# Phases and coarse decays of an S4D convolution kernel as one row-tiled product

## The chip, the cores and the metric

The kernel runs on one core of a Trainium2 chip. The metric is the device time of one execution in microseconds; before the change it was 622.47 us, the median of three runs (621.3 to 626.9). TensorE multiplies, VectorE (DVE), ScalarE (ACT) and GpSimd (POOL) do element-wise work, SyncE (SP) issues nearly all transfers.

## The reference

Two branches of the same width are computed in float32 and mixed by a gate; L = 2048 steps, D = 640 channels, N = 128 modes, Dff = 1728.

```
g = sigmoid((u * gate_w).sum(-1))
dt = exp(log_dt);  A = -exp(log_A_real) + 1j*A_imag;  C = (C_real + 1j*C_imag) * dt
K[d, l] = 2 * Re( sum_n C[d, n] * exp(A[d, n] * dt[d] * l) )
a = causal convolution of u with K over l (by FFT) + u * D_skip
b = relu(x @ w1) @ w2
out = g * a + (1 - g) * b
```

## The kernel before

**Three kinds of work share TensorE.** The feed-forward branch (PSUM tile `pf`, called fill below) is computed in three parts of w1 and w2, each operand split into a high and a low half: products of 512 columns into the hidden layer, products of 320 columns out of it. Generation builds the filters K. The convolution (PSUM tile `pc`) transforms filters and input, multiplies and transforms back; it can only open when generation is over and its memory is free.

**Generation** goes through the 640 channels in 40 groups of 16. For each channel, step l is split as a coarse step of 32 and a fine rest, so that the exponential is a product of few values. Each channel has eight rows of parameters in tile `PS` (high and low halves of the phase per step, its offset, the decay, the size), 16 channels by 8 rows filling its 128 partitions; the modes are its columns. A visit of group c multiplies `PS` (stationary) by a table `tg` that holds the step numbers, spread so that each row only meets the columns of its own channel (`spread`, line 952). Before the change a visit is five products of 512 columns: two for the phases (`phases`, line 1018, tile `pg`: 16 channels of 64 values, two PSUM banks), two for the coarse decays (`exponents`, line 1041, tile `px`, the same size, two banks) and one for the fine decays (tile `pe`, 16 by 32, one bank).

Then ACT rounds the phases to an integer (`cs<-pg`), DVE subtracts it (`sn<-pg,cs`, line 1035) and takes the magnitude, ACT takes the exponential of the fine decays (`me<-pe`) and the coarse ones (`mg<-px`, line 1059), loads its other table and takes sine and cosine; DVE multiplies these into factors (`factors`, line 1075). Two groups at a time are then multiplied with each other (`taps`, tile `pk`, 128 small products), turned by DVE into `kt` and stored. The program has one `pk` for each of 20 pairs of groups.

**The convolution** takes 128 channels at a time, i = 0 to 4: a transform of the filter and of the input (tables `tf`, 64x64 tiles of TensorE's array), a second one (`tm`, 64x32 tiles), products by ACT, DVE and POOL, the inverse (`inv2`, table `tn`, 32x64 tiles), two copies by ACT (`back`), eight transposes by DVE (`relay`, line 1331), the last transform (`inv1`, table `tw`) and multiplication by the gate (ACT, tile `yo`).

**Mixing.** `CG` (line 23) has one entry for each of eight row blocks g of 256 steps. For the first CG[g] of the five channel blocks, the branch b of row block g takes the finished a (`joined`, `with_last`); for the others, b is stored to `py`, and a takes it when it is ready (POOL adds `yj` or `xu` to `yo`).

**The order of the work** is made when the program is built: a planner (`Plan.run`, line 226) has for each task an engine, an estimated duration, its dependencies, tokens of the buffers that it takes (`tok`) and a rank, and writes each engine's instructions in the order that comes out. Each engine runs its own in that order; only waits on others move them in time. TensorE changes between modes ('f' for full products, 't' and 'c' for tiles), which the planner prices. The layer below adds the waits between engines from the tiles that instructions share.

Of the kernel before, what the change touches and what calls it, by code (L numbers as in the profile page):

```python
# [10 lines left out]
F32 = mybir.dt.float32  # L11
F32R = mybir.dt.float32r
I32 = mybir.dt.int32
AF = mybir.ActivationFunctionType
# [5 lines left out]
NT = D // 128  # L20
TWO_PI = 2 * math.pi
PARTS = (5, 5, 4)
CG = (0,0,0,0,1,2,5,5)
FIRST = 7
SPIN = 6
S4R = 3
# [22 lines left out]
TGA = 4  # L49
# [4 lines left out]
GPR = 1  # L54
# [16 lines left out]
def slots():  # L71
    return np.concatenate([np.arange(32, 64), np.arange(31, -1, -1)])
# [5 lines left out]
def tables():  # L78
    a = np.arange(64)
    k1 = 2 * np.arange(32)[None, :] + np.arange(2)[:, None]  # L80
    al = 2 * np.pi * (k1[..., None] + 0.25) * a / 64
    f1 = np.stack([np.cos(al), np.sin(al)]).transpose(3, 1, 0, 2).reshape(64, 128)
    w = np.stack([np.cos(al), np.sin(al)], axis=1) / 2048
    b = np.arange(32)
    om = 2 * np.pi * (k1[:, :, None, None] + 0.25 + 64 * b[None, None, :, None]) * b / 2048
    c, s = np.cos(om), np.sin(om)
    m = np.zeros((2, 2, 32, 32, 2, 32))
    n = np.zeros((4, 32, 8, 2, 2, 2, 32))
    for p in range(2):
        ct, st = c[p].transpose(2, 0, 1), s[p].transpose(2, 0, 1)  # L90
        m[p, 0, :, :, 0], m[p, 0, :, :, 1] = ct, st
        m[p, 1, :, :, 0], m[p, 1, :, :, 1] = -st, ct
        for g in range(32):
            ck, sk = c[p, g], s[p, g]
            n[g % 4, :, g // 4, p, 0] = np.stack([ck, -sk], axis=1)
            n[g % 4, :, g // 4, p, 1] = np.stack([sk, ck], axis=1)


    tg = np.zeros((16, 8, 176))
    tg[:, :2, :32], tg[:, :2, 32:64], tg[:, 2:4, :32] = b, 32 * b + 16, 1  # L100
    tg[:, 4:6, 64:128], tg[:, 4:6, 128:160], tg[:, 6:, 128:160] = 32 * slots(), b, 1
    tg[np.arange(16), :, 160 + np.arange(16)] = 1
    f = lambda x: np.ascontiguousarray(x.astype(np.float32))
    return dict(t_g=f(tg.reshape(128, 176)), t_f1=f(np.tile(np.stack([f1, f1[slots()]], axis=1), (2, 1, 1))), t_w=f(w.reshape(128, 64)),
                t_m=f(m.reshape(128, 32, 64)), t_n=f(n.reshape(128, 8, 2, 2, 64)))


# [245 lines left out]
class Kernel:  # L353
# [30 lines left out]
    def feed_forward(self):  # L384
# [276 lines left out]
        def with_y(g, q_, qld):  # L661
            n, ts = CG[g], []
            for t in range(2):
# [6 lines left out]
        def joined(g, t, q_, dep):  # L670
            b, m, ts = 2 * g + t, min(CG[g], 4), []
            if m:
# [64 lines left out]
        for p, n in enumerate(PARTS):  # L737
# [4 lines left out]
            for k, g in enumerate(order):  # L742
# [84 lines left out]
    def params(self):  # L827
        tc, nc, io, A = self.tc, self.nc, self.io, self.plan.add
        V, S, P, D_ = self.V, self.S, self.P, self.D
        tl, last = {}, {}  # L830
# [66 lines left out]
        R = lambda f: (lambda V: f(V, *T_()))  # L897
# [48 lines left out]


        def steps_in():
            tl['tgs'] = self.prm.tile([128, 176], F32, name="tgs")
            D_.dma_start(tl['tgs'], io['t_g'])  # L950

        def spread(ds):
            def go():
                a, b = self.tg[:, :2048].rearrange("p (x d j) -> p d x j", x=2, j=64), self.tg[:, 2048:].rearrange("p (d j) -> p d j", j=32)
                for d in ds:
                    m = tl['tgs'][:, 160 + d:161 + d]
                    S.mul(a[:, d], tl['tgs'][:, :128].rearrange("p (x j) -> p x j", x=2), m)
                    S.mul(b[:, d], tl['tgs'][:, 128:160], m)
            return go
        a = A('SP', 'tg', 0.62, steps_in, [self.prm0], kb=88, rank=TGR)  # L960
        if TGR > 5:
            self.late_loads.append(a)
        for d in range(0, 16, 2):
            self.tg_done.append(A('ACT', 'tg', 1.1, spread(range(d, d + 2)), [a], rank=TGA))
        return [*done, *self.tg_done]

    def ssm(self, C=16):
        tc, nc, io, A, tok, ring = self.tc, self.nc, self.io, self.plan.add, self.plan.token, self.plan.ring
        V, S, P, D_ = self.V, self.S, self.P, self.D
        Q, n = C // 4, D // C  # L970
# [7 lines left out]
        self.tg = gk.tile([128, 2560], F32R, name="tg")  # L978
# [13 lines left out]
        st = {}  # L992
# [4 lines left out]
        opened = self.prm_shut = A('PY', 'open', 0, go, self.params())  # L997
        self.prm_open = opened
        R, rows = {}, {}
# [12 lines left out]
                rows[c + k] = a, r_  # L1012

        tasks, f = {}, {}
        I = lambda x: x.bitcast(I32)


        def phases(c):
            p_, s_ = tok('pg'), tok('sc')
            rd, r_ = rows[c]  # L1020

            def pe():
                p = self.psg.tile([128, 4, 256], F32, name="pg")
                pf = p.rearrange("p d j -> p (d j)")
                st['pg'] = pf.rearrange("p (d j) -> p d j", j=64)
                for h in range(2):
                    x = slice(h * 512, h * 512 + 512)
                    self.E.matmul(pf[:, x], R[c], self.tg[:, x], start=True, stop=True)

            def whole():  # L1030
                st['sc', c] = [st['gp'].tile([128, C, 64], F32, name=k, bufs=5) for k in ("sn", "cs")]
                S.copy(I(st['sc', c][1]), st['pg'])
            a = visit[c, 1] = A('PE', None, 0.46, pe, [rd, opened, *self.tg_done], take=[p_], use=[r_], rank=GPR, mode='f')
            b = acts[c, 0] = A('ACT', None, 0.97, whole, [a], take=[s_], use=[p_], rank=2)
            d = A('DVE', 'g1', 1.14, lambda: V.tensor_sub(st['sc', c][0], st['pg'], I(st['sc', c][1])), [b],
                  use=[p_, s_], rank=G1R)
            e = A('DVE', 'g1', 0.62, lambda: V.tensor_scalar(I(st['sc', c][1]), I(st['sc', c][0]), 0x7fffffff, None,
                                                             op0=ALU.bitwise_and), [d], use=[s_], rank=G1R, port=True)
            tasks[c] = dict(s=s_, abs=e)

        def exponents(c):
            p_, m_ = tok('px'), tok('mg')
            rd, r_ = rows[c]

            def pe():
                p = self.psg.tile([128, 4, 256], F32, name="px")
                pf = p.rearrange("p d j -> p (d j)")
                st['px', c] = pf.rearrange("p (d j) -> p d j", j=64)
                for h in range(2):
                    x = slice(h * 512, h * 512 + 512)  # L1050
                    self.E.matmul(pf[:, x], R[c], self.tg[:, 1024 + h * 512:1536 + h * 512], start=True, stop=True)
                q = st['pe', c] = self.psg.tile([128, C, 32], F32, name="pe")
                self.E.matmul(q.rearrange("p d j -> p (d j)"), R[c], self.tg[:, 2048:], start=True, stop=True)

            def exps(k):
                def go():
                    if k:
                        st['mg', c] = st['gp'].tile([128, C, 64], F32, name="mg", bufs=4)
                        S.activation(st['mg', c], st.pop(('px', c)), AF.Exp)
# [13 lines left out]
            tasks[c].update(m=m_, exps=[d, b], trig=[x, y])  # L1073
# [65 lines left out]
        visit, acts = {}, {}  # L1139
# [16 lines left out]
        for p in range(n // 2 + 1):  # L1156
            c = 2 * p
# [349 lines left out]
```

## Time and profile before

| | before |
|---|---|
| median of 3 runs | 622.47 us |
| the profiled execution | 632.85 us, span 631.1 us |
| TensorE busy | 609.0 us (97%), 7864 matmuls |
| VectorE busy | 507.9 us (80%) |
| ScalarE busy | 399.0 us (63%) |
| GpSimd busy | 92.4 us (15%) |
| granted TensorE clock, mean | 0.992 |
| first product of generation, last `pk` product begins | 82.7 us, 402.4 us |
| last product with `tw` begins | 608.3 us |

A TensorE row's duration runs from its start to a modelled end, and neighbours overlap; what a product costs is read from the distance of starts. The span is from the first to the last instruction; the profiled execution's own time has 1.8 us around it. Names such as `pf<-xx,w1h` are out<-in by the program's tile names.

### The profile page before, as it was taken

How to read it: one execution, taken by the hardware profiler on the slowest of the kernel's cores; microseconds unless marked ns; L12 is line 12 of the kernel's file. 1: busy time of each engine (PE TensorE's matmuls, PEld its weight loads, DVE VectorE, ACT ScalarE, POOL GpSimd, SP SyncE). 2: the span in 40 equal slices, each digit the busy share in tenths (PEclk: the TensorE clock that was granted, in tenths of full speed). 3: DMA queues.
4: the chain of work that ended last, by engine and by line, in shares of the span. 5: the costliest groups of instructions: out<-in, count | busy, mean ns of one | idle time of the engine just before them, and what ended most of it. 6: DMA issues, size and time to landing. Idle time of an engine off the chain costs nothing.

```text
span 631.1 us, 18316 instructions
## 1 busy us (share of the span) xinstructions
PE 609.0 (97%) x7864; PEld 481.6 (76%) x7864; DVE 507.9 (80%) x794; ACT 399.0 (63%) x579; POOL 92.4 (15%) x133
## 2 busy tenths in 40 slices
PE   7999989999999999999999999999979999989997
PEld 5998969888988988988988988755656465656656
DVE  5998559898999889999999998568676757746842
ACT  6578369997999888788789796023225342342470
POOL 0000000000000000000000000007060180361744
PEclk9999989998999999999999999999999999999999
DMA  9993933913656435535442243781543534563343
GB/s 292 386 371 116 406 102 115 301 58 109 195 184 242 153 108 205 153 112 177 133 144 81 64 162 116 234 339 30 194 127 126 183 103 136 185 221 102 115 149 119
DMA packets 54153, 108.05 MB, mean 171 GB/s; under 512 B 5432, under 2 KB 29880, under 8 KB 53176
## 3 DMA queue, kind: packets, MB, share of 16 engines
q1 hardware_dynamic: 53848, 106.63, 50.4%
q8 instruction: 62, 1.02, 0.7%
q10 hardware_dynamic: 224, 0.25, 0.1%
q14 instruction: 19, 0.16, 0.1%
HBM read 67.79 MB, written 39.06 MB: 169 GB/s over the span
## 4 chain that ended last, share of the span: by engine, by line
PE 78%; DVE 11%; DMA 5%; ACT 3%; issue 2%; POOL 0%; SPq 0%; DVEq 0%; ACTq 0%
PE pf L322 47%; PE pc L322 18%; PE pk L322 6%; PE pg L322 3%; PE px L322 2%; PE pe L322 1%; DMA ws<-in_B_w_dram 1%; DVE hwl L322 1%; DVE mg L322 1%; DVE sn L322 1%; DVE G L322 1%; DMA ps<-hl 1%; DMA xu<-in_x_dram 1%; DMA ws<-in_w_dram 1%; DMA PS<-ps 1%
## 5 line engine op out<-in xcount | busy, mean ns | idle before, releaser
L322 PE MATMUL pf<-xx,w1h 128*128 128x512 f32 x560 | 175.5, 399 | 1.7 <-DVE w1h L322 1.0
L322 PEld LDWEIGHTS pf<-xx,w1h 128*128 128x128 f32 x560 | 102.6, 189 | 37.2 <-issue 12.6
L322 PE MATMUL pf<-xx,w1l 128*128 128x512 f32 x260 | 102.1, 393 | 0.0
L322 ACT COPY ku<-pc 128x512 f32<-128x512 f32 (+1 forms) x60 | 43.8, 758 | 74.0 <-PE pc L322 63.4
L322 POOL TENSOR_TENSOR ku<-ku 128x256 f32<-128x256 f32 x80 | 56.2, 744 | 86.2 <-DVE ku L322 56.8
L322 POOL TENSOR_TENSOR kt<-kt,dsk 128x8 f32<-128x8 f32 x20 | 9.3, 466 | 393.0 <-DVE kt L322 211.6
L322 DVE STREAM_TRANSPOSE ku<-pc 128x512 f32<-128x512 f32 x80 | 50.8, 687 | 15.4 <-PE pc L322 15.2
L322 DVE TENSOR_TENSOR ku<-pc,ku 128x512 f32<-128x512 f32 x80 | 52.8, 686 | 11.0 <-ACT ku L322 9.6
L322 PE MATMUL pf<-w2l,hh 128*128 128x320 f32 x192 | 59.2, 312 | 1.9 <-issue 1.9
L322 PE MATMUL pf<-w2h,hh 128*128 128x320 f32 x192 | 59.7, 315 | 0.8 <-DVE q L322 0.8
L322 PE MATMUL pf<-w2h,hwh 128*128 128x320 f32 x192 | 59.7, 312 | 0.7 <-ACT hwh L322 0.7
L322 PE MATMUL pf<-w2l,hwh 128*128 128x320 f32 x192 | 59.9, 313 | 0.0
L322 PE MATMUL pf<-w2h,hwl 128*128 128x320 f32 x192 | 58.1, 316 | 1.9 <-DVE hwl L322 1.9
L322 ACT CAST cs<-pg 128x1024 int32<-128x1024 f32 x40 | 40.4, 1010 | 29.5 <-PE pg L322 29.4
L322 PEld LDWEIGHTS pf<-xx,w1l 128*128 128x128 f32 x260 | 49.0, 188 | 11.0 <-DVE w1l L322 0.3
L322 DVE TENSOR_TENSOR sn<-pg,cs 128x1024 f32<-128x1024 f32 x40 | 48.6, 1215 | 7.5 <-ACT cs L322 7.4
L322 ACT ACT_TABLE_LOAD x42 | 53.9, 1283 | 0.7
L322 DVE TENSOR_TENSOR mg<-mg,cs 128x1024 f32<-128x1024 f32 x40 | 49.0, 1224 | 2.9 <-ACT cs L322 1.0
L322 PE MATMUL pf<-w2h,hl 128*128 128x320 f32 x160 | 48.1, 317 | 0.0
L322 ACT ACTIVATE cs<-cs,half_pi 128x1024 f32<-128x1024 f32 x40 | 45.7, 1142 | 0.0
L322 PE MATMUL pc<-ku,tm 64*32 64x256 f32 x1280 | 42.9, 392 | 2.7 <-issue 2.4
L322 ACT ACTIVATE mg<-px 128x1024 f32<-128x1024 f32 x40 | 41.3, 1033 | 1.8 <-PE pk L322 1.8
(151 smaller groups left out, 1260.4 us busy)
## 6 DMA issues: line engine op xcount, KB each, us to landing
xx<-xt SPq DMA_DIRECT2D x24, 640.0 KB, 4.7
xt<-xx SPq DMA_DIRECT2D x16, 640.0 KB, 8.8
part<-q SPq DMA_DIRECT2D x16, 640.0 KB, 3.3
q<-part SPq DMA_DIRECT2D x16, 640.0 KB, 4.9
xl<-in_u_r_dram SPq DMA_DIRECT2D x16, 320.0 KB, 3.1
kd<-kt SPq DMA_DIRECT2D x80, 64.0 KB, 2.5
xu<-in_u_b_dram SPq DMA_DIRECT2D x5, 1024.0 KB, 4.9
xu<-in_x_t_dram SPq DMA_DIRECT2D x6, 640.0 KB, 6.8
```

What stands on the lines that cost most here:

```text
L322: self._last = self._tc.keep_in_program_order(f(*a, **k))
```

## The change

The sixteen channels of a group stand as four sets of four, each set on 32 partitions of `PS`. The table `tg` shrinks from 2560 to 1024 columns: columns 0 to 255 hold the phase steps of four channels, 256 to 511 the coarse decay steps, and every set of 32 rows finds its own four channels there; columns 512 to 1023 hold the fine decays as before. A visit is now four products of 32 rows, 128 columns of weights and 512 moving columns, each on its own quarter of the array's rows and into its own PSUM bank, then the one product for `pe`. Tile `pg` has four banks; in each, the first half is phases, the second coarse decays. Tile `px` is gone; `pg` alone takes the four banks that both had. The token of the old `px` is taken together with that of `pg`. The planner is told 0.26 us and mode 'g' for the four products and 0.24 us for the fifth. The table is written by 20 ACT instructions in place of 32. `CG[6]` goes from 5 to 3. The rest of the program's text is unchanged, but the planner lays it out anew.

```
-CG = (0,0,0,0,1,2,5,5)
+CG = (0, 0, 0, 0, 1, 2, 3, 5)
...
-    tg = np.zeros((16, 8, 176))
+    tg = np.zeros((16, 8, 180))
...
+    tg[np.arange(16), :, 176 + np.arange(16) % 4] = 1
...
-                    m = tl['tgs'][:, 160 + d:161 + d]
-                    S.mul(a[:, d], tl['tgs'][:, :128].rearrange("p (x j) -> p x j", x=2), m)
-                    S.mul(b[:, d], tl['tgs'][:, 128:160], m)
+                    if d < 4:
+                        S.mul(a[:, d], tl['tgs'][:, :128].rearrange("p (x j) -> p x j", x=2), tl['tgs'][:, 176 + d:177 + d])
+                    S.mul(b[:, d], tl['tgs'][:, 128:160], tl['tgs'][:, 160 + d:161 + d])
...
         def phases(c):
             p_, s_ = tok('pg'), tok('sc')
+            px_ = pxs[c] = tok('px')
...
-                p = self.psg.tile([128, 4, 256], F32, name="pg")
-                pf = p.rearrange("p d j -> p (d j)")
-                st['pg'] = pf.rearrange("p (d j) -> p d j", j=64)
-                for h in range(2):
-                    x = slice(h * 512, h * 512 + 512)
-                    self.E.matmul(pf[:, x], R[c], self.tg[:, x], start=True, stop=True)
+                p = self.psg.tile([128, 4, 512], F32, name="pg")
+                st['pg'], st['px', c] = p[:, :, :256], p[:, :, 256:]
+                for m in range(4):
+                    x = slice(32 * m, 32 * m + 32)
+                    self.E.matmul(p[:, m], R[c][x], self.tg[x, :512], start=True, stop=True)
...
-            a = visit[c, 1] = A('PE', None, 0.46, pe, [rd, opened, *self.tg_done], take=[p_], use=[r_], rank=GPR, mode='f')
+            a = visit[c, 1] = A('PE', None, 0.26, pe, [rd, opened, *self.tg_done], take=[p_, px_], use=[r_], rank=GPR, mode='g', n=4)
...
-                p = self.psg.tile([128, 4, 256], F32, name="px")
...
-                    self.E.matmul(pf[:, x], R[c], self.tg[:, 1024 + h * 512:1536 + h * 512], start=True, stop=True)
...
-            a = visit[c, 2] = A('PE', None, 0.69, pe, [rd, opened, *self.tg_done], take=[p_], use=[r_], rank=GPR, mode='f')
+            a = visit[c, 2] = A('PE', None, 0.24, pe, [rd, opened, *self.tg_done], use=[p_, r_], rank=GPR, mode='f', n=1)
```

In the order of the built programs, three places matter. First TensorE, a visit in the middle of generation; before:

```order
L322 MATMUL pf<-xx,w1h_1657 128x512 x2
L322 MATMUL pf<-xx,w1l_1658 128x512
L322 MATMUL pg<-tg,PS 128x512 x2
L322 MATMUL px<-tg,PS 128x512 x2
L322 MATMUL pe<-tg,PS 128x512
L322 MATMUL pf<-xx,w1h_1683 128x512 x2
```

A visit in the changed program, also between rows of fill:

```order
L323 MATMUL pf<-w2l_2148,hwh_2213 128x320
L323 MATMUL pf<-w2h_2147,hwl_2214 128x320
L323 MATMUL pg<-tg,PS 128x512 x4
L323 MATMUL pe<-tg,PS 128x512
L323 MATMUL pf<-w2h_1933,hh_1981 128x320
L323 MATMUL pf<-w2l_1934,hh_1981 128x320
```

The four rows of `pg` and `px` became four row-tiled ones; the number of products is the same. Around the visits, fill moved: ahead of the last `pk` stand 640 products of 512 columns and 1010 of 320 in the old program, 682 and 1024 in the new one. Second ACT, one group after another in generation, with the engines that each row waits for; before:

```order
L322 CAST cs<-pg 128x1024 [waits Activation_49]
L322 ACT_TABLE_LOAD
L322 ACTIVATE me<-pe 128x512 [waits Activation_49]
L322 ACTIVATE mg<-px 128x1024 [waits Activation_49]
L322 CAST cs<-pg 128x1024 [waits PE_49,Activation_49]
L322 ACTIVATE me<-pe 128x512 [waits PE_49]
L322 ACTIVATE mg<-px 128x1024
```

In the changed program, where `mg<-pg` reads the second half of the four banks:

```order
L323 CAST cs<-pg 128x1024 [waits PE_49]
L323 ACT_TABLE_LOAD
L323 ACTIVATE me<-pe 128x512 [waits PE_49]
L323 ACTIVATE mg<-pg 128x1024 [waits DVE_49,PE_49]
L323 ACTIVATE hh_2612<-pf 128x512 [waits PE_49]
```

A wait of the exponential for DVE is new. The value waited for is the subtraction `sn<-pg,cs` of the same group, for 30 of the 40 groups; for the other ten it is the subtraction that waits for the exponential. In the old program neither waits for the other. Third TensorE at the end, around the last product with `tw`; before:

```order
L322 MATMUL pf<-xx,w1h_4326 128x512 x2
L322 MATMUL pf<-xx,w1l_4327 128x512
L322 MATMUL pc<-ku,tw 64x512 x8
L322 MATMUL pf<-w2h_4675,hh_7429 128x320
L322 MATMUL pf<-w2l_4676,hh_7429 128x320
```

And in the changed program:

```order
L323 MATMUL pf<-w2l_4632,w2h_7452 128x320
L323 MATMUL pf<-w2h_4631,w2l_7453 128x320
L323 MATMUL pc<-ku,tw 64x512 x8
L323 MATMUL pf<-w2h_4489,hh_7044 128x320
L323 MATMUL pf<-w2l_4490,hh_7044 128x320
```

Behind the last `tw`, 96 products of 320 columns are left in the old program (row blocks 6 and 7), 24 in the new one. Between the last inverse (`tn`) and that `tw`, the old program has fifteen products of 512 columns plus three and the `tw` of the block before, the new one 24 products of 320 columns alone.

More of the change, by code (lines that the diff above doesn't have):

```diff
@@ L102, in tables @@
     tg[np.arange(16), :, 160 + np.arange(16)] = 1
+    tg[np.arange(16), :, 176 + np.arange(16) % 4] = 1
     f = lambda x: np.ascontiguousarray(x.astype(np.float32))
-    return dict(t_g=f(tg.reshape(128, 176)), t_f1=f(np.tile(np.stack([f1, f1[slots()]], axis=1), (2, 1, 1))), t_w=f(w.reshape(128, 64)),
+    return dict(t_g=f(tg.reshape(128, 180)), t_f1=f(np.tile(np.stack([f1, f1[slots()]], axis=1), (2, 1, 1))), t_w=f(w.reshape(128, 64)),
                 t_m=f(m.reshape(128, 32, 64)), t_n=f(n.reshape(128, 8, 2, 2, 64)))
@@ L948, in steps_in @@
         def steps_in():
-            tl['tgs'] = self.prm.tile([128, 176], F32, name="tgs")
+            tl['tgs'] = self.prm.tile([128, 180], F32, name="tgs")
             D_.dma_start(tl['tgs'], io['t_g'])
@@ L953, in go @@
             def go():
-                a, b = self.tg[:, :2048].rearrange("p (x d j) -> p d x j", x=2, j=64), self.tg[:, 2048:].rearrange("p (d j) -> p d j", j=32)
+                a, b = self.tg[:, :512].rearrange("p (x d j) -> p d x j", x=2, j=64), self.tg[:, 512:].rearrange("p (d j) -> p d j", j=32)
                 for d in ds:
-                    m = tl['tgs'][:, 160 + d:161 + d]
-                    S.mul(a[:, d], tl['tgs'][:, :128].rearrange("p (x j) -> p x j", x=2), m)
-                    S.mul(b[:, d], tl['tgs'][:, 128:160], m)
+                    if d < 4:
+                        S.mul(a[:, d], tl['tgs'][:, :128].rearrange("p (x j) -> p x j", x=2), tl['tgs'][:, 176 + d:177 + d])
+                    S.mul(b[:, d], tl['tgs'][:, 128:160], tl['tgs'][:, 160 + d:161 + d])
             return go
@@ L962, in params @@
             self.late_loads.append(a)
-        for d in range(0, 16, 2):
-            self.tg_done.append(A('ACT', 'tg', 1.1, spread(range(d, d + 2)), [a], rank=TGA))
+        for d in range(0, 16, 4):
+            self.tg_done.append(A('ACT', 'tg', 1.1 if d else 2.2, spread(range(d, d + 4)), [a], rank=TGA))
         return [*done, *self.tg_done]
@@ L977, in ssm @@
         self.gw = gk.tile([128, D], F32, name="gw")
-        self.tg = gk.tile([128, 2560], F32R, name="tg")
+        self.tg = gk.tile([128, 1024], F32R, name="tg")
         dsk = gk.tile([128, n // 2, 2 * Q], F32, name="dsk")
@@ L1014, in ssm @@
         tasks, f = {}, {}
+        pxs = {}
         I = lambda x: x.bitcast(I32)
+        quads = lambda x: x.rearrange("p (m d) j -> p m (d j)", m=4)
         def phases(c):
             p_, s_ = tok('pg'), tok('sc')
+            px_ = pxs[c] = tok('px')
             rd, r_ = rows[c]
             def pe():
-                p = self.psg.tile([128, 4, 256], F32, name="pg")
-                pf = p.rearrange("p d j -> p (d j)")
-                st['pg'] = pf.rearrange("p (d j) -> p d j", j=64)
-                for h in range(2):
-                    x = slice(h * 512, h * 512 + 512)
-                    self.E.matmul(pf[:, x], R[c], self.tg[:, x], start=True, stop=True)
+                p = self.psg.tile([128, 4, 512], F32, name="pg")
[3 more added lines that the diff above has]
+                    self.E.matmul(p[:, m], R[c][x], self.tg[x, :512], start=True, stop=True)
             def whole():
                 st['sc', c] = [st['gp'].tile([128, C, 64], F32, name=k, bufs=5) for k in ("sn", "cs")]
-                S.copy(I(st['sc', c][1]), st['pg'])
-            a = visit[c, 1] = A('PE', None, 0.46, pe, [rd, opened, *self.tg_done], take=[p_], use=[r_], rank=GPR, mode='f')
+                S.copy(quads(I(st['sc', c][1])), st['pg'])
+            a = visit[c, 1] = A('PE', None, 0.26, pe, [rd, opened, *self.tg_done], take=[p_, px_], use=[r_], rank=GPR, mode='g', n=4)
             b = acts[c, 0] = A('ACT', None, 0.97, whole, [a], take=[s_], use=[p_], rank=2)
-            d = A('DVE', 'g1', 1.14, lambda: V.tensor_sub(st['sc', c][0], st['pg'], I(st['sc', c][1])), [b],
+            d = A('DVE', 'g1', 1.14, lambda: V.tensor_sub(quads(st['sc', c][0]), st['pg'], quads(I(st['sc', c][1]))), [b],
                   use=[p_, s_], rank=G1R)
@@ L1041, in exponents @@
         def exponents(c):
-            p_, m_ = tok('px'), tok('mg')
+            p_, m_ = pxs[c], tok('mg')
             rd, r_ = rows[c]
             def pe():
-                p = self.psg.tile([128, 4, 256], F32, name="px")
[L1047 to L1050, printed above, removed]
-                    self.E.matmul(pf[:, x], R[c], self.tg[:, 1024 + h * 512:1536 + h * 512], start=True, stop=True)
                 q = st['pe', c] = self.psg.tile([128, C, 32], F32, name="pe")
-                self.E.matmul(q.rearrange("p d j -> p (d j)"), R[c], self.tg[:, 2048:], start=True, stop=True)
+                self.E.matmul(q.rearrange("p d j -> p (d j)"), R[c], self.tg[:, 512:], start=True, stop=True)
             def exps(k):
@@ L1058, in go @@
                         st['mg', c] = st['gp'].tile([128, C, 64], F32, name="mg", bufs=4)
-                        S.activation(st['mg', c], st.pop(('px', c)), AF.Exp)
+                        S.activation(quads(st['mg', c]), st.pop(('px', c)), AF.Exp)
                     else:
```

## The prediction

> **What bounds the kernel now.** I read the page's head first, then the chain that ended last, then three stretches: generation (from the first `pg` to the last `pk`), the convolution up to its last `tw` product, and the end.
>
> ```profile
> span 631.1 us, 18316 instructions
> PE 609.0 (97%) x7864; PEld 481.6 (76%) x7864; DVE 507.9 (80%) x794; ACT 399.0 (63%) x579; POOL 92.4 (15%) x133
> PE 78%; DVE 11%; DMA 5%; ACT 3%; issue 2%; POOL 0%; SPq 0%; DVEq 0%; ACTq 0%
> ```
>
> ```profile
> core 0: us, PE busy (x) PEld busy (x) DVE busy (x) ACT busy (x) POOL busy (x), PEclk, DMA share, GB/s
> 82.70:402.60 319.90, 317.06 (x4016) 279.30 (x4016) 295.65 (x437) 269.69 (x315) 9.12 (x19) 0.99 0.45 147
> 402.60:608.30 205.70, 197.23 (x3334) 119.97 (x3332) 143.07 (x230) 75.83 (x147) 71.85 (x96) 0.99 0.47 154
> 608.30:631.10 22.80, 18.14 (x113) 15.09 (x112) 5.01 (x9) 4.83 (x17) 10.56 (x11) 1.00 0.47 156
> ```
>
> TensorE sets the pace in all three. But generation is the stage that the change touches, and there DVE is busy 295.65 of 319.9 us (92%) and ACT 269.69 (84%): DVE has 24 us to spare and ACT 50, spread over 20 pairs of groups (1.2 and 2.5 us a pair). So a shorter visit is worth its time only while neither of the two is pushed to the end of its reserve. Part of ACT's reserve is waiting for the visits themselves:
>
> ```profile
> ACT cs L322 <- PE pg L322: 29.4, 16, 3.8
> ```
>
> **The visit.** Starts of successive rows on TensorE, a visit between rows of fill:
>
> ```profile
> 212.07 0.31 PE L322 MATMUL pf<-w2l,hh 128*128 128x320 f32 x1
> 212.22 0.62 PE L322 MATMUL pg<-tg,PS 128*128 128x512 f32 x2
> 212.68 0.62 PE L322 MATMUL px<-tg,PS 128*128 128x512 f32 x2
> 213.14 0.40 PE L322 MATMUL pe<-tg,PS 128*128 128x512 f32 x1
> 213.38 0.31 PE L322 MATMUL pf<-w2h,hl 128*128 128x320 f32 x1
> ```
>
> Five products take 213.38 - 212.22 = 1.16 us, 0.23 each. Four row-tiled ones are not in this trace with 128 columns of weights, but the inverse has the nearest form: 32-row tiles, four side by side in four banks.
>
> ```profile
> L322 PE MATMUL pc<-ku,tn 32*64 32x128 f32 x1280 | 22.8, 276 | 3.8 <-issue 3.8
> L322 PE MATMUL pc<-xu,tf 64*64 64x512 f32 x160 | 19.1, 601 | 0.0
> ```
>
> An instruction of the inverse lasts 276 ns but costs 22.8/1280 = 18 ns of busy time; one of 64x64 tiles with 512 columns lasts 601 ns and costs 119. So tiles do overlap, with their weight loads. I take 0.23 for the four. What is added is the change of mode, there and back:
>
> ```profile
> 220.73 0.39 PE L322 MATMUL pf<-xx,w1l 128*128 128x512 f32 x1
> 221.05 0.32 PE L322 MATMUL pk<-mg,cs 128*32 128x64 f32 x8
> ...
> 206.04 0.29 PE L322 MATMUL pk<-G,sn 128*32 128x64 f32 x8
> 206.27 0.42 PE L322 MATMUL pf<-w2l,hwh 128*128 128x320 f32 x1
> 206.52 0.31 PE L322 MATMUL pf<-w2h,hwl 128*128 128x320 f32 x1
> 206.67 0.31 PE L322 MATMUL pf<-w2h,hwh 128*128 128x320 f32 x1
> ```
>
> Into tiles: 221.05 - 220.73 - 0.23 = 0.09 us. Out of them: eight `pk` take 0.11, so 206.27 - 206.04 - 0.11 = 0.12; and the first full product then stands 0.25 before its follower where 0.15 is usual, 0.10 for a weight load of 128 columns that nothing hides. The `pk` loads of 32 columns are shorter, so I add 0.07 at the entry. The visit: 0.09 + 0.07 + 0.23 + 0.12 + 0.10 + 0.23 (`pe`) = 0.84. Saved: 0.32 x 40 visits = **12.8 us** of TensorE. Bounds: 20.4 with the changes of mode at half (0.19 of the 0.38, a visit of 0.65), and -14.8 if the four products stand in a row (0.92 for 0.23, a visit of 1.53); if only their weight loads do (three more of 0.10, a visit of 1.14), 0.8.
>
> The Trainium skill ("TensorE: Matmul & The Clock Gate", Measured speedup vs the span model) gives four 32-row tiles of 512 columns a speedup of 3.07. By that the four would take 0.92/3.07 = 0.30, an estimate, and the sum below would be 2.8 us worse; no run shows this form yet.
>
> **What the fill does with it.** A product of 320 columns costs 0.146 us, by 22 distances from the first to the last of these rows (23 products):
>
> ```profile
> 623.68 0.30 PE L322 MATMUL pf<-w2l,hh 128*128 128x320 f32 x1
> ...
> 626.90 0.31 PE L322 MATMUL pf<-w2h,w2l 128*128 128x320 f32 x1
> ```
>
> Ahead of the last `pk` the order has 42 more products of 512 columns and 14 more of 320: 42 x 0.23 + 14 x 0.146 = 11.7 us of fill pulled into generation. Generation by TensorE alone: -12.8 + 11.7 = **-1.1 us**. For DVE and ACT that fill is little:
>
> ```profile
> L322 DVE SCALAR_TENSOR_TENSOR hwl<-pf,hwh 128x512 fp32r<-128x512 f32 x24 | 16.4, 685 | 2.7 <-ACT hwh L322 2.7
> L322 ACT ACTIVATE hwh<-pf 128x512 fp32r<-128x512 f32 x24 | 14.2, 590 | 3.7 <-PE pf L322 3.5
> ```
>
> One of each for 15 products of 512 columns, so about 2 us for the 42.
>
> **The new wait.** Phases and coarse decays now lie in the same banks, and the order shows the exponential `mg` behind the subtraction `sn<-pg,cs` for 30 groups, the subtraction behind the exponential for ten. In the old trace they overlap. The first and the last of the 40 groups, exponential and subtraction:
>
> ```profile
> 86.73 1.02 ACT L322 ACTIVATE mg<-px 128x1024 f32<-128x1024 f32 x1
> 84.95 1.23 DVE L322 TENSOR_TENSOR sn<-pg,cs 128x1024 f32<-128x1024 f32 x1 [4.16 <-ACT cs L322]
> ...
> 378.53 1.00 ACT L322 CAST cs<-pg 128x1024 int32<-128x1024 f32 x1
> 379.92 1.03 ACT L322 ACTIVATE mg<-px 128x1024 f32<-128x1024 f32 x1
> 380.24 1.22 DVE L322 TENSOR_TENSOR sn<-pg,cs 128x1024 f32<-128x1024 f32 x1
> ```
>
> In the first the subtraction ended before the exponential began: 0. In the last it ended at 381.46, 1.54 after it began. Summed over the 40 it is 25.0 us, nearly all in the second group of a pair, where no table load stands between `cs` and `me`; about 1.25 a pair. Half of ACT's reserve of 2.5 covers that in the 30 groups where ACT waits. DVE has less: its subtraction can start only when `me` and `mg` are through (in the last rows 380.95 - 379.53 = 1.42 us after `cs` ends), where it began a median of 0.45 after it in those ten groups (0.71 in the last rows); at most 1.0 for each of the ten. The order has them there because DVE was to come late, so I take 0.65 each, **+6.5 us**, as if all of DVE's landed and ACT's were hidden. Queued behind: on DVE the factors that `taps` needs, on ACT the table load, the sines and the next `cs`, on TensorE the next visit, which needs all four banks free. Ends: 0 (hidden: 24 and 50 us are free) and 25.0 (all lands). A gain is excluded, since nothing starts earlier for it.
>
> The Trainium skill has a rule that speaks against this placement ("PSUM — Partial Sum Buffer", PSUM bank collisions raise a hardware error): two engines must not touch one bank on the same partitions at once, reads included. The new wait in the order agrees; with `px` in banks of its own there was none.
>
> **The convolution.** Between the last `pk` and the last `tw` stand 180 products of 512 and 206 of 320 columns in the old order, 138 and 264 in the new: 71.7 against 70.5 us, **-1.2**. Its own work is the same.
>
> **The end.** Between the last inverse and the last `tw` lie ACT's copies and DVE's transposes:
>
> ```profile
> 598.03 3.03 PE pc L322 x128
> 600.07 2.07 ACT L322 COPY ku<-pc 128x1024 f32<-128x1024 f32 x2 [2.20 <-issue]
> 602.24 4.87 DVE L322 STREAM_TRANSPOSE ku<-ku 128x512 f32<-128x512 f32 x8 [4.99 <-ACT ku L322]
> 608.32 3.58 PE pc L322 x16
> ```
>
> From 600.0, where the inverse is through and ACT's copies begin, to 607.1 is 7.1 us. Fill and other `tw` covered it; in the new order only 24 products, 24 x 0.146 = 3.5, do. TensorE idles **+3.6**.
>
> Behind the last `tw`, 96 products (14.1 us) become 24 (3.5), since row block 6 no longer waits for the last channel blocks. Then the other chain ends last: gate, joins, store.
>
> ```profile
> 609.43 3.20 ACT L322 ACTIVATE yo<-pc,gate 128x128 f32<-128x128 f32 x12 [0.47 <-PE pc L322]
> 612.44 1.23 ACT L322 ACTIVATE ku<-pc,gate 128x128 f32<-128x128 f32 x4
> 610.65 3.78 POOL L322 TENSOR_TENSOR yo<-yo,xu 128x512 f32<-128x512 f32 x3 [3.64 <-ACT yo L322]
> 623.98 0.89 POOL L322 TENSOR_TENSOR q<-q,ku 128x128 f32<-128x128 f32 x2
> 627.32 0.55 DVE L322 SCALAR_TENSOR_TENSOR q<-pf,omg,q 128x320 f32<-128x320 f32 x1 [1.21 <-PE pf L322]
> ```
>
> Counted from the start of the last `tw` at 608.3: POOL's three joins ran 2.4 to 6.1; a fourth of half size adds 0.65, the two `q<-q,ku` now behind it 0.9, DVE 0.55, and from DVE's start to the span's end are 631.1 - 627.3 = 3.8 with that 0.55: 6.1 + 0.65 + 0.9 + 3.8 = 11.5. SP has three more stores in its queue ahead of the last, of which I take 0.5. So 12.0 in place of 22.8: **-10.8** (between -9 and -11.5). Twelve ACT instructions of the table's making go too (5 us at about 45 to 55 us), beside fill that keeps TensorE fed; 0, and at most 2 (the wait of the first `pg`).
>
> **The sum.** -1.1 + 6.5 - 1.2 + 3.6 - 10.8 = -3.0 us, against the profiled 632.85. The median is 10.4 us lower; I carry the difference over as it is: 622.5 - 3.0 = 619.5, say **619**.
>
> **Rivals.**
> A. The waits are hidden: 24 us of DVE and 50 of ACT suffice, and the 6.5 fall away. 622.5 - 9.5 = 613. For it: the plan kept TensorE at 99% of generation with DVE at 92%. Against: DVE takes its instructions in order.
> B. The waits land whole: every us that an exponential or subtraction is late delays the pair, since with 25 us of waiting ACT would be taken for 93% of a generation of 319 us, DVE is at 93%, and each waits for the other. 622.5 - 9.5 + 25 = **638**, slower. It decides from 9.5/40 = 0.24 us a group: above that the change loses.
> C. The four weight loads go one after another (0.30 more a visit): 12 us on top, 631: the change would not do what it says. Against: the 18 ns of the inverse.
>
> A fifth possibility, a worse end or stalls elsewhere, gets what remains.
>
> **How the numbers follow.** Forecast (615 to 624) 0.42, A (609 to 615.9) 0.27, B (627 to 640) 0.20, C 0.08, rest 0.03. One per cent, about what a measurement can tell here, is 6.2 us: below 616.2 is faster. Faster: A and a seventh of the forecast, 0.33. Same: the rest of the forecast and 0.02, 0.38. Slower: B, C and 0.01, 0.29. The range 608 to 632 leaves out most of B and little of A, about 0.2.
>
> **What would show it.** A visit of 0.84 us between fill rows; more than 1.15 says that tiles or loads stand in a row. `mg<-pg` idle before it by DVE `sn`: 10 to 15 us in all with generation ending near 408 is my case; near 401 is A; over 420 is B. The last `tw` 12 us before the end, with POOL and the stores of `yo` last; an idle stretch of some 3.6 us ahead of it. Wrong would be the sum if the convolution, with another order of its parts, idled more than its 8.5 us.

## The result

The changed kernel takes 630.96 us (median of 20 runs, 627.99 to 641.84), the kernel before 628.2 us on the same chips (median of 20, 621.3 to 630.88): a ratio of 1.0061 with a 95% interval of 1.0035 to 1.0086 (here and below, ratios leave out disturbed executions and are not the quotient of the medians). It is slower by 0.6%, about 3.8 us by that ratio and 2.8 us by the medians, which lies within the 1% that a few runs can tell; with 20 runs on each side the interval leaves out a gain. The forecast was a gain of 3.0 us. The first three runs of before, 622.47, were at the low end of what it does.

The page's head of the changed kernel, with the share of the chain that ended last in its last line:

```profile
span 629.6 us, 18249 instructions
PE 593.4 (94%) x7864; PEld 456.2 (72%) x7864; DVE 506.4 (80%) x794; ACT 397.2 (63%) x567; POOL 93.4 (15%) x133
PE 65%; DVE 18%; ACT 8%; DMA 4%; issue 4%; POOL 0%; POOLq 0%; SPq 0%; DVEq 0%; ACTq 0%
```

TensorE lost 15.6 us of busy time (609.0 to 593.4) and yet the span fell by 1.5 only. DVE's and ACT's shares of the last chain went from 11% and 3% to 18% and 8%: TensorE waits for them now. The three stages of the changed kernel, in the columns of the table by stretches (length, then busy time of each engine, clock, DMA share, GB/s):

```profile
83.90:414.00 330.10, 314.47 (x4071) 263.05 (x4071) 297.32 (x441) 275.64 (x321) 10.06 (x19) 1.00 0.44 148
414.00:617.30 203.30, 193.76 (x3356) 120.18 (x3347) 143.11 (x232) 72.31 (x142) 75.52 (x100) 0.99 0.46 154
617.30:629.60 12.30, 7.37 (x40) 4.73 (x40) 1.93 (x4) 4.23 (x16) 6.98 (x8) 0.99 0.60 197
```

Generation grew from 319.9 to 330.1 us. TensorE is busy there 2.6 us less than before (317.06 to 314.47) and idle 12.8 us more (2.8 to 15.6). The convolution is 2.4 us shorter than in the profile before, the end 10.5 us. So the place to look is generation, and in it what TensorE and ACT waited for:

```profile
PE pg L323 <- ACT mg L323: 5.3, 9, 1.3
PE pg L323 <- DVE sn L323: 5.0, 9, 0.8
ACT mg L323 <- DVE sn L323: 10.4, 13, 1.3
DVE sn L323 <- ACT mg L323: 6.2, 8, 1.1
```

(Columns: us in all, times, longest.) Ahead of 18 of the 40 visits TensorE stood, 10.3 us together, until the exponential or the subtraction of the group before had let go of the four banks; in the profile before, such a wait came once, 0.6 us. That is 9.7 of the 12.8 us.

One caution on the numbers before. Its profiled execution took 632.85 us, 4.6 above its median; that of the changed kernel, 631.36, is at its own. Run 3 below has before's order up to the end and gives a second execution to compare with.

### The profile page after: what moved, and what is told of

It reads as the page before. It is cut to its first block, busy times and chain, and to the rows that moved or that the text cites. A ratio compares the mean times of both kernels' runs of the same rounds, so it can differ in the third digit from the quotient of the medians.

```text
span 629.6 us, 18249 instructions
## 1 busy us (share of the span) xinstructions
PE 593.4 (94%) x7864; PEld 456.2 (72%) x7864; DVE 506.4 (80%) x794; ACT 397.2 (63%) x567; POOL 93.4 (15%) x133
## 4 chain that ended last, share of the span: by engine, by line
PE 65%; DVE 18%; ACT 8%; DMA 4%; issue 4%; POOL 0%; POOLq 0%; SPq 0%; DVEq 0%; ACTq 0%
PE pf L323 41%; PE pc L323 17%; DVE sn L323 5%; PE pk L323 4%; DVE ku L323 2%; ACT mg L323 2%; DMA xl<-in_u_r_dram 2%; ACT cs L323 2%; PE pg L323 2%; DVE G L323 2%; DVE cs L323 2%; DVE mg L323 1%; PE pe L323 1%; ACT L323 1%; DVE hwl L323 1%
## 5 line engine op out<-in xcount | busy, mean ns | idle before, releaser
L323 PEld LDWEIGHTS pf<-xx,w1h 128*128 128x128 f32 x560 | 103.5, 189 | 33.5 <-issue 10.4
L323 POOL TENSOR_TENSOR kt<-kt,dsk 128x8 f32<-128x8 f32 x20 | 10.3, 513 | 403.5 <-DVE kt L323 252.8
L323 PEld LDWEIGHTS pf<-xx,w1l 128*128 128x128 f32 x260 | 49.1, 189 | 11.2 <-DVE w1l L323 0.6
L323 ACT CAST cs<-pg 128x1024 int32<-128x1024 f32 x40 | 40.4, 1010 | 26.2 <-PE pg L323 23.4
L323 ACT ACTIVATE mg<-pg 128x1024 f32<-128x1024 f32 x40 | 41.2, 1029 | 12.0 <-DVE sn L323 10.4
```

The lines of the kernel that those rows point to most:

```text
L323: self._last = self._tc.keep_in_program_order(f(*a, **k))
```

## The experiments

**1. No wait.** The coarse exponential reads the bank of the fine decays (each value twice) in place of the second half of the four banks. Same number and size of instructions and the same order on every engine. It leaves out the use of the coarse decays.

```
-  S.activation(quads(st['mg', c]), st.pop(('px', c)), AF.Exp)
+  S.activation(st['mg', c].rearrange("p d (h j) -> p d h j", h=2), st.pop(('pe', c))[:, :, None].to_broadcast([128, C, 2, 32]), AF.Exp)
```

> The changed kernel with the coarse exponential fed from the bank of the fine decays (the same number of elements, each read twice; its values are wrong, so what is left out is the use of the coarse decays). Every engine's order stays as it is; only the wait between exponential and subtraction is gone. If that wait is what cost generation its gain: TensorE's idle time before `pg` falls from about 10 us to under 3, the last `pk` ends at 402 to 405 us instead of 414, and the kernel takes 619 to 622. If the fill that was pulled into generation, or the row tiles themselves, are the cause: 629 to 631 as the changed kernel, and the last `pk` stays near 412.

619.73 us beside 628.12, a ratio of 0.9899 (0.9838 to 0.996). Its stages:

```profile
83.70:402.00 318.30, 314.24 (x4072) 264.21 (x4072) 297.10 (x441) 273.64 (x321) 9.69 (x19) 0.99 0.47 153
402.00:604.20 202.20, 194.58 (x3353) 121.28 (x3349) 143.22 (x232) 72.40 (x142) 75.91 (x100) 0.99 0.47 156
604.20:618.40 14.20, 10.15 (x40) 5.45 (x40) 1.81 (x4) 4.50 (x16) 6.69 (x8) 0.74 0.47 156
```
```profile
PE pg L323 <- DVE sn L323: 0.8, 1, 0.8
```

TensorE's busy time in generation is the changed kernel's to 0.2 us, and its idle time 4.1 in place of 15.6, with 0.8 us left ahead of `pg`: generation is **11.8 us** shorter, and the whole time 11.2 (by the medians, and by the spans of the two profiles). Without the exponential's read of these banks the kernel is 1% faster than before; with it, it is 0.6% slower. The edit takes away two things at once: the waits of ACT and DVE for each other, and the exponential's hold on banks that the next visit must write. Runs 5, 6 and 10 try to tell these apart.

**2. Shared banks alone.** Before's five full products in before's order, but with phases and coarse decays in the two halves of the same four banks. No row tiles, no new `CG`.

```
-  p = self.psg.tile([128, 4, 256], F32, name="px")
...
+  p = st['four'] = self.psg.tile([128, 4, 512], F32, name="pg")
+  st['pg'], st['px', c] = p[:, :, :256], p[:, :, 256:]
```

> The kernel before with its five full products and its own order, but with phases and coarse decays in halves of the same four banks: the wait without the row tiles. If the wait is the cause by itself: TensorE idles 6 us or more before `pg`, and the kernel is 6 to 12 us slower than before (634 to 640). If the wait only hurts in the new layout of the work, or is hidden: within 2 us of before (626 to 630).

647.95 us, a ratio of 1.0367 (1.0277 to 1.0458): 20 us, more than I expected. Generation and its waits:

```profile
82.10:419.30 337.20, 320.46 (x4016) 276.93 (x4016) 297.20 (x437) 271.85 (x315) 9.14 (x19) 0.99 0.43 139
```
```profile
PE pg L322 <- ACT mg L322: 8.7, 11, 2.1
PE pg L322 <- DVE sn L322: 3.7, 5, 0.9
ACT cs L322 <- PE pg L322: 34.9, 20, 3.9
```

The loss appears without any row-tiled product. It is the placement in the banks, not the tiles. One more thing comes with this placement: the rounding now needs all four products, where before it needed the first two, and ACT waits 34.9 us for the visits in place of 29.4. So the 20 us are the price of the placement as a whole, not of the wait between the two readers alone.

**3. New `CG` alone.** Before, with `CG` 3 for row block 6 and nothing else.

```
-CG = (0,0,0,0,1,2,5,5)
+CG = (0, 0, 0, 0, 1, 2, 3, 5)
```

> The kernel before with the new CG alone. By the prediction's terms the shorter end (-10.8) is paid by fill that must run earlier (+10.6), and the idle stretch ahead of the last `tw` (+3.6) comes on top: 630 to 634, 2 to 6 us slower than before. If the shorter end is a gain of its own: 618 to 624.

627.39 us beside 628.12, a ratio of 1.0015 (0.9973 to 1.0056): no difference, where I had expected a loss. All engines have before's order up to the last stretch, so its first two stages are a second execution of before's:

```profile
83.50:400.70 317.20, 314.38 (x4016) 276.41 (x4016) 295.55 (x437) 269.44 (x315) 9.15 (x19) 1.00 0.46 148
400.70:600.70 200.00, 195.42 (x3332) 119.07 (x3330) 142.95 (x230) 75.99 (x147) 71.98 (x96) 0.99 0.48 156
600.70:629.40 28.70, 18.23 (x113) 15.14 (x112) 5.11 (x9) 4.84 (x17) 10.55 (x11) 0.86 0.46 147
```

Generation took 317.2 here and 319.9 in the profile I predicted from, the convolution 200.0 and 205.7. Against this second execution the changed kernel's generation is 12.9 us longer, and its convolution 3.3 longer rather than 2.4 shorter. With before's products, 96 of the fill are still behind the last `tw`, and the end is 28.7 us, no shorter. Its granted clock was 0.86 there, in the end of the profile before 1.00, so the two ends are not quite comparable.

**4. Tiles with the old `CG`.** The changed kernel with `CG` 5 for row block 6, the edit of 3 reversed.

> The change with CG as before (5 for row block 6). Theory: the loss lies in generation, so it stays (last `pk` ends 8 us or more later than before), and the end is that of before, with some 20 us from the last `tw` to the end and no idle stretch ahead of it: 624 to 631. If the new CG were the cause of the loss: 618 or less.

639.68 us, a ratio of 1.0214 (1.0134 to 1.0294): missed, well above. Generation is as in the changed kernel, the end is not:

```profile
83.20:413.70 330.50, 316.01 (x4072) 264.27 (x4072) 297.21 (x441) 275.42 (x321) 10.08 (x19) 0.99 0.45 148
413.70:621.00 207.30, 197.30 (x3351) 121.43 (x3349) 143.04 (x231) 72.43 (x142) 73.46 (x97) 0.98 0.45 150
621.00:641.00 20.00, 10.52 (x40) 6.66 (x40) 2.11 (x4) 4.46 (x16) 9.12 (x10) 0.74 0.35 119
```

In this layout the new `CG` is worth about 9 us; in before's (run 3) nothing. The amount of fill is not the reason: the rows of TensorE and DVE come in the changed kernel's order, with the same 24 products of fill behind the last `tw`. With `CG` 5 row block 6 waits there for the last channel block, which POOL joins, and DVE and TensorE for POOL:

```profile
631.37 1.01 DVE L323 SCALAR_TENSOR_TENSOR q<-pf,omg,q 128x320 f32<-128x320 f32 x2 [10.56 <-POOL q L323]
631.98 0.64 PE L323 MATMUL pf<-w2h,hh 128*128 128x320 f32 x1 [5.67 <-DVE q L323]
```

The clock of this end was 0.74. It was 0.74 in run 1 too, with the changed kernel's rows, and the end took 14.2 us there; the other 5.8 us are about TensorE's 5.67 us of standing. So some 6 of the 9 us are the new `CG`'s; the rest, with a convolution 4.0 us longer than the changed kernel's in the same order of TensorE's rows, is not explained. In before's end, TensorE has 96 products to do meanwhile. So the end's gain belongs to the two edits together.

**5. Exponentials first.** The changed kernel with ACT's order `me`, `mg`, then `cs`, so that no exponential stands between rounding and subtraction in either direction.

```
-  ... (c, 0), (c, 1), (c, 2), (c + 1, 0), (c + 1, 1), (c + 1, 2)]
+  ... (c, 1), (c, 2), (c, 0), (c + 1, 1), (c + 1, 2), (c + 1, 0)]
```

> The changed kernel with ACT's order of a group turned round: fine and coarse exponential first, then the rounding, so that the subtraction comes behind all three and neither engine waits for the other in the middle. The banks are shared as before and stay taken through me, mg, cs and sn in series (0.5 + 1.0 + 1.0 + 1.2 us). If the cost is that ACT and DVE stand still for each other: most of it is back, the last pk ends at 403 to 407 us, the kernel takes 620 to 625. If the cost is only how long the four banks stay taken: TensorE still idles about 10 us before pg and the kernel takes 628 to 632.

637.88 us, a ratio of 1.019 (1.0064 to 1.0316): both of my numbers missed. Waits of ACT and DVE, and generation:

```profile
ACT me L323 <- PE pe L323: 52.5, 18, 4.6
DVE sn L323 <- ACT cs L323: 20.3, 16, 3.3
```
```profile
83.40:425.80 342.40, 339.29 (x4221) 288.88 (x4221) 302.90 (x453) 277.75 (x329) 9.47 (x19) 1.00 0.48 158
```

Now ACT waits 52.5 us for the visits and DVE 20.3 for ACT. TensorE hardly waits, because the plan put another 150 products of fill into generation: its busy time there is 24.8 us more than in the changed kernel (339.29 against 314.47), twice what generation grew by. Two things changed here, the order of the readers and the layout of the fill, so this run does not decide what costs, the two readers' waits or the time that the banks stay taken. It shows that this order, in which rounding, subtraction and exponential still stand in a row on one set of banks, is no way out.

**6. The planner told.** The changed kernel with the exponential's wait as a dependency of the plan, so that it lays out the order knowing it.

```
-  d = acts[c, 2] = A('ACT', None, 0.96, exps(1), [b], use=[p_, m_], rank=2, mode='exp')
+  d = acts[c, 2] = A('ACT', None, 0.96, exps(1), [b, tasks[c]['sub']], use=[p_, m_], rank=2, mode='exp')
```

> The changed kernel with one more dependency in the planner: the coarse exponential comes behind the subtraction of its group. The wait is the same; only the layout of the work knows of it. If the cost is mostly that the order was made without the wait: the idle time before pg falls to some 4 us and the kernel takes 622 to 627. If the wait itself costs the time whatever the order: 629 to 634.

628.32 us beside 626.68, a ratio of 1.0062 (1.0018 to 1.0106), the changed kernel's; the time fell between the two expectations.

```profile
82.40:414.40 332.00, 324.87 (x4130) 273.71 (x4130) 299.92 (x446) 276.97 (x323) 10.29 (x19) 0.99 0.46 152
```
```profile
ACT mg L323 <- DVE sn L323: 20.5, 20, 1.6
PE pg L323 <- ACT mg L323: 2.0, 1, 2.0
```

TensorE's waits went from 10.3 to 2.0 us, since fill took their place (59 more products than in the changed kernel's generation), while ACT's doubled, and generation, 332.0 us, is no shorter than the changed kernel's 330.1. A plan that knows of the wait fills it; it does not make the pair shorter.

**7. Two tiles, banks apart.** Row tiles of 64 rows, two for the phases in two banks, two for the coarse decays in two others, with the new `CG`. Nothing is shared, and the fill ahead of the last `pk` is before's (640 products of 512 columns, 1010 of 320).

```
-  p = self.psg.tile([128, 4, 512], F32, name="pg")
+  p = st['pg'] = self.psg.tile([128, 2, 512], F32, name="pg")
...
+  p = st['px', c] = self.psg.tile([128, 2, 512], F32, name="px")
+  for m in range(2):
+      x = slice(64 * m, 64 * m + 64)
+      self.E.matmul(p[:, m], R[c][x], self.tg[x, 512:1024], start=True, stop=True)
```

> Row tiles of 64 in place of 32 rows: eight channels a product, two side by side for the phases in two banks of their own, two for the coarse decays in two others (table of 1536 columns), then the fine decays; CG as in the change. A visit should be one product longer than the changed one, 1.00 us against 0.77, and no wait between exponential and subtraction is left. If the wait is the whole loss: the last pk ends near 407 us, 40 x 0.23 = 9 us later than without the wait or less, and the kernel takes 622 to 629. If row tiles cost something else: over 630.

634.68 us, a ratio of 1.0152 (1.0057 to 1.0247). By the two cases set down, that is the second: something other than the wait costs time here.

```profile
83.30:398.50 315.20, 312.09 (x4015) 258.91 (x4015) 294.87 (x437) 269.94 (x315) 9.48 (x19) 0.99 0.46 149
398.50:606.20 207.70, 198.72 (x3344) 119.79 (x3336) 142.94 (x230) 77.29 (x148) 71.96 (x96) 0.98 0.47 153
606.20:633.30 27.10, 17.57 (x109) 14.52 (x108) 5.10 (x9) 4.33 (x17) 10.52 (x11) 0.88 0.41 136
```

Generation is 2.0 us shorter than in run 3, with no wait for banks to speak of. A visit takes 1.09 us with its entry, 0.07 less than before's, so there is little to gain (40 x 0.07 = 2.8). So that cost does not lie in generation. What follows takes the gain back: a convolution of 207.7 and an end of 27.1 us with 92 products of fill behind the last `tw`. Why the convolution is 7.7 us longer than run 3's, this run does not show.

**8 and 9. Two tiles with `CG` 5 and 4 for row block 6.**

> Two tiles of 64 rows, phases and decays in banks of their own, and row block 6 as it was before the change (CG 5). Theory (the shared banks are what the change loses by; the tail of the run with two tiles was the order at the end alone, 27.1 us behind the last transform with 92 products of fill in it): generation as there, 315 us, 4 to 5 shorter than before the change, and an end of 20 to 23 us: 622 to 626 beside 628 before. Rival (what TensorE saves in generation never comes out, since the same fill has to be done later): 627 to 631. In the run with four tiles the old CG cost 9 us; if that holds here too, 640.

> As the run with two tiles, with CG 4 for row block 6: the last channel block alone is joined late there. Generation does not know of it, 315 us again. If the end goes by how much fill is left behind the last transform, it comes to between that of CG 3 (27.1 us) and what CG 5 gives; 622 to 632 in all. No theory of the waits tells these apart: this one shows how far the end moves by the plan alone.

631.99 and 630.05 us beside 623.44, ratios of 1.0103 (1.0059 to 1.0147) and 1.0111 (1.0071 to 1.0151). The ends are short again (22.2 and 22.5 us), and generation is 314.2 and 316.0; but the convolution takes 212.0 and 206.0. So the first theory was right in generation and end and wrong in the sum. The rival's 627 to 631 us is nearer to both times, but its reason does not fit: the stage of generation holds before's number of products (4016), so no fill was left over for later. In both the convolution idles for 3 to 4 us at one `tw` that waits for ACT:

```profile
PE pc L323 <- ACT yo L323: 3.8, 1, 3.8
```

(This is the run with `CG` 5.) That is part of the 6 to 12 us by which these convolutions exceed run 3's; the rest was not taken apart. Banks apart did not make a faster kernel in any of the three runs, and why is open.

**10. Halves.** The changed kernel with its four banks as two PSUM tiles, `pg` and `ph`, of two banks each; rounding, subtraction and coarse exponential become two instructions of half the size.

```
-  p = self.psg.tile([128, 4, 512], F32, name="pg")
+  p = [self.psg.tile([128, 2, 512], F32, name=k) for k in ("pg", "ph")]
...
+  for h in range(2):
+      S.activation(half(st['mg', c], h), q[h], AF.Exp)
```

> The changed kernel with the four banks as two PSUM tiles of two banks each, and rounding, subtraction and coarse exponential each as two instructions of half the size, so that the exponential of the first half can run beside the subtraction of the second. Same products, same bytes; 80 more instructions on ACT (about 0.16 us each by 1.02 us for 1024 columns against 0.59 for 512: 12.8 us of its 50 free) and 40 more on DVE (about 0.1 each, 4 us of its some 20 free). Theory (the loss is the time that a group holds its four banks, rounding, subtraction and exponential in series): the series shortens by about 1 us a group, TensorE's waits ahead of a visit go from 10 us to under 4, generation from 330 to 321 to 325, the time to 621 to 626 beside 628 before. Rival (DVE and ACT are at their limit and any added instruction shows): generation 330 to 336, 631 to 637.

627.64 us beside 625.61, a ratio of 1.006 (1.0014 to 1.0105), the changed kernel's. Generation, TensorE's wait, and one group:

```profile
84.20:409.80 325.60, 319.64 (x4072) 266.52 (x4072) 299.69 (x481) 280.23 (x401) 9.71 (x19) 0.99 0.46 150
```
```profile
PE pg L323 <- ACT mg L323: 1.7, 2, 1.3
```
```profile
141.39 0.63 ACT L323 ACTIVATE mg<-pg 128x512 f32<-128x512 f32 x1
141.87 0.65 ACT L323 ACTIVATE mg<-ph 128x512 f32<-128x512 f32 x1
142.06 0.69 DVE L323 TENSOR_TENSOR sn<-pg,cs 128x512 f32<-128x512 f32 x1 [0.41 <-ACT mg L323]
142.66 0.68 DVE L323 TENSOR_TENSOR sn<-ph,cs 128x512 f32<-128x512 f32 x1
```

The subtraction of the first half runs beside the exponential of the second. TensorE's waits went from 10.3 to 1.7 us, as expected, and generation from 330.1 to 325.6, just short of the expected 321 to 325; the whole time did not move beside the kernel before. Its profiled execution (623.44 us) lies 4.2 us below its median, so the profile flatters it. Of generation's 11.8 us the halves give back 4.5. The extra instructions cost DVE 2.4 us of busy time in the stage (the two half subtractions stand 0.60 us apart, so 1.28 in place of 1.22) and ACT 4.6. TensorE's busy time rose by 5.2 us with the same products (314.47 to 319.64), so not all that its waits lost was won; why is not shown.

No complete kernel among these is faster than the one before.

## Why the prediction was wrong

**The visit: near.** The rows around one visit of the changed kernel that did not wait:

```profile
217.99 0.39 PE L323 MATMUL pf<-xx,w1l 128*128 128x512 f32 x1
218.31 0.51 PE L323 MATMUL pg<-tg,PS 32*128 32x512 f32 x4
218.74 0.50 PE L323 MATMUL pe<-tg,PS 128*128 128x512 f32 x1
219.08 0.63 PE L323 MATMUL pf<-xx,w1h 128*128 128x512 f32 x2
```

The entry takes 218.31 - 217.99 - 0.23 = 0.09, the four tiles with the way out of them 0.43, `pe` with its weight load 0.34: **0.86**, predicted 0.84. The 0.07 for the weight load at the entry was not there, and the tiles took 0.08 more than the 0.23 + 0.12. The visits between fill rows that did not wait, 17 of the 40, agree with this one: 0.77 us from `pg` to the next fill, plus the entry. Less the 0.12 for the way out, the four took 0.31; the estimate from the Trainium skill ("TensorE: Matmul & The Clock Gate", Measured speedup vs the span model), 0.30, was nearer than the 0.23 that I took from the inverse. The saving is 12.0 us for 12.8. Rival C (weight loads in a row) is out.

**The new wait: the step that failed.** I took 6.5 us, "as if all of DVE's landed and ACT's were hidden". Without the dependency generation is 11.8 us shorter (run 1); by TensorE's sum, -12.0 + 11.7 = -0.3 against a measured growth of 10.2 to 12.9, it is 10.5 to 13.2. DVE's part was about right: 6.2 us in eight groups, though "at most 1.0 for each" was read from a median (in the profile before, the subtraction began as early as 0.03 us after the rounding in one of the ten, which makes 1.4). ACT waited 10.4 us in 13 of the 30 groups. That is the size that I had named as the sign of my case (10 to 15 us, generation ending near 408); but generation ended at 414. So the wait was sized about right, and what failed is that ACT's part would be hidden: behind it stood the visit. How, these rows show:

```profile
218.87 1.01 ACT L323 CAST cs<-pg 128x1024 int32<-128x1024 f32 x1 [0.53 <-PE pg L323]
220.34 1.22 DVE L323 TENSOR_TENSOR sn<-pg,cs 128x1024 f32<-128x1024 f32 x1
221.59 1.02 ACT L323 ACTIVATE mg<-pg 128x1024 f32<-128x1024 f32 x1 [1.21 <-DVE sn L323]
222.67 0.50 PE L323 MATMUL pg<-tg,PS 32*128 32x512 f32 x4 [0.68 <-ACT mg L323]
```

Rounding, subtraction and exponential follow one another, 3.7 us from 218.87 to 222.6, and only then may TensorE write the four banks again. Over the rows of all 40 groups it is 4.0 us on average, and in run 1, where only rounding and subtraction read these banks, 2.65. Before, the subtraction and the exponential read different banks and each pair of banks came free by itself. ACT's reserve, which I set against the wait as a mean per pair, was not where the wait fell: it lay largely in ACT's wait for the visits (`cs` behind `pg`, 29.4 us before, 23.4 after), which now come late themselves. I named "the next visit, which needs all four banks free" as queued behind, and gave it no price. How much of the 11.8 us is the two readers' standing for each other and how much the longer hold is not separated by these runs; run 10 takes 4.5 us back by shortening both. Rival B had the right mechanism, each engine late for the other, with too high a price (25 us, all of the overlap). Rival A's price, 9.5 us off, is near what run 1 shows without the wait: 8.4 us, 1.0% of the time.

**What decides: half right.** The point from which the change loses, 0.24 us a group, was the right yardstick. 11.8/40 is 0.30, and the kernel is a little slower.

**Convolution and end: the shapes right, the base one long execution.** The idle stretch ahead of the last `tw` and what came behind it:

```profile
613.52 0.31 PE L323 MATMUL pf<-w2h,w2l 128*128 128x320 f32 x1
617.30 1.08 PE L323 MATMUL pc<-ku,tw 128*64 128x512 f32 x4 [3.47 <-DVE ku L323]
...
619.69 4.46 POOL L323 TENSOR_TENSOR yo<-yo,xu 128x512 f32<-128x512 f32 x4 [0.69 <-ACT yo L323]
624.10 0.87 POOL L323 TENSOR_TENSOR q<-q,ku 128x128 f32<-128x128 f32 x2
625.01 0.55 DVE L323 SCALAR_TENSOR_TENSOR q<-pf,omg,q 128x320 f32<-128x320 f32 x1 [1.44 <-POOL q L323]
```

TensorE idles from 613.67 to 617.30, 3.6 us as predicted, and the end takes 12.3 us (12.0 predicted), with POOL's joins and the stores last. But the convolution of the profile before was 5.7 us longer than that of run 3 with the same order. Against run 3 it is +3.3 us, where -1.2 + 3.6 = +2.4 was predicted. Put together against run 3's first two stages and before's own end: generation +12.9, convolution +3.3, end -10.5, a start 0.4 later: +6.1 us by single executions, where the ratio gives +3.8 and the medians +2.8. With the wait at 11.8 in place of 6.5, and 0.8 less saved by the visits, the prediction's own sum would have been +3.1.

**The base.** "I carry the difference over as it is" took 10.4 us off a profile on the strength of three runs. Over 20 runs the median is 4.6 us below that profile. The sum's sign does not hang on this, the predicted time of 619 does: the same -3.0 from 628.2 gives 625.2.

## What to carry to other kernels

When two results that different engines read are put into the same PSUM banks, price more than the two readers' mutual wait: add up how long the banks stay taken, reader after reader, and ask who must write them next. A reserve of an engine over a whole stage may hide nothing if it consists of waiting for that very producer. Before stage lengths of one profiled execution are used as a base, compare its time with the median, since here two executions of one order differed by 5.7 us in one stage.

## What the runs showed that I had not expected

Sharing four banks between two readers, alone, cost 20 us (run 2), more than the 11.8 us that it costs in the changed kernel; why more is not shown, but in run 2 the rounding also has to wait for two products more. The same `CG` edit is worth nothing in one layout (run 3) and about 9 us in the other (run 4). And a convolution in one order of instructions took 205.7 us in one execution and 200.0 in another, at a granted clock of 0.99 in both; in the first, TensorE's idle time that the profile calls issue, ahead of `pc`, was 6.2 us, in the second 1.9:

```profile
PE pc L322 <- issue: 6.2, 5, 3.2
PE pc L322 <- issue: 1.9, 1, 1.9
```

What lies behind those stretches, the profile does not show.
